# Two layers of spectral mixing and MLP on one core: layer 2's d transform by frequency modulo four, split halves on the way back, and some work on GpSimd

## The chip, the cores and the metric

The kernel runs on one core of a Trainium2 chip. The core has TensorE (PE in the profile; its weight loads are listed as PEld), VectorE (DVE), ScalarE (ACT), GpSimd (POOL) and a queue engine (SP), each with its own instruction stream; they meet only through semaphores. The metric is device time in microseconds, the median of several executions. Matrix products take a stationary operand of 128 columns (a weight load) and stream a moving operand of up to 512 columns past it; results land in PSUM, which has eight banks of 512 fp32 per partition, and DVE or ACT copy them from there to SBUF.

## The reference

One sequence of S = 2048 rows of D = 512 columns in bf16 goes through two identical layers. Each layer is a spectral block and a mixer-MLP block, both with residuals:

```python
def _A_ref(x, w_r, w_i):
    X = jnp.fft.rfft2(x.astype(jnp.float32), axes=(-2, -1))
    X = X * (w_r + 1j * w_i)
    return jnp.fft.irfft2(X, s=(S, D), axes=(-2, -1)).astype(jnp.bfloat16)

def _B_ref(x, w1, w2, w3, w4):
    h = gelu(layernorm(x) @ w1)
    # four column groups of h, shifted by +1, -1, +2, -2 rows: g0..g3
    x1 = x + concatenate([g0, g1, g2, g3]) @ w2
    return x1 + gelu(layernorm(x1) @ w3) @ w4

for layer in range(2):
    x = x + _A_ref(layernorm(x), A_w_r, A_w_i)
    x = x + _B_ref(layernorm(x), B_w1, B_w2, B_w3, B_w4)
```

w1 and w2 are 512x512, w3 is 512x1792, w4 is 1792x512. The spectral weights have 2048x257 entries and are the same in both layers.

## The kernel before

Row 16p+q of x is held in partition p, slot q (`K.x`, 128 x 16 x 512), so the row transform over 2048 points splits into one of 128 points over p and one of 16 points over q. Each layer runs these stages; in brackets is the letter by which an order list calls them.

- Front (O, G): for each slot q the table T, scaled by the row's 1/std (Q, `scaled_T`), is the moving operand and x[:, q] the stationary one. The result, transposed to d on the partitions, goes to V (`take_V`). There are three forms of the matmuls. `over_p_quarters` (line 431) makes eight a row, of 256 and 128 columns, and delivers four combinations of the four quarters of d. `over_p` (413, 415) makes four of 256 columns and delivers the sums and differences of the two halves of d. `over_p_plain` (441) makes four of 128 columns; ACT then copies the right half (`right`) and DVE folds it with the left (`fold_V`, four additions, line 453). Layer 1's front, at the start of the kernel, uses the quarters for all rows. Layer 2's front, in the last part of layer 1, uses the plain form for the first five pairs of rows (PLAIN = 5) and `over_p` for two pairs and two single rows.
- d transform (d, t): `over_d` makes four matmuls for each of 16 blocks b. Layer 1 (lines 549, 551, 555) takes frequencies modulo four, with the table FL: two matmuls of 128 and two of 256 columns. Layer 2 (line 560) takes even and odd frequencies, with the table FA: four of 256 columns. `take_d` copies PSUM to TV on ACT (line 159) or DVE (157). Blocks 2 to 13 go in pairs, 0, 1, 14 and 15 singly (UNITS).
- q transform (q, x): `over_q` (584), and the copy to X by `take_q`. X has two buffers.
- Weights (p): `weigh` (603) multiplies X by the real and imaginary planes of W on DVE, into PB.
- q back (b, m): `back_q` (614), eight matmuls of 128 columns a block, and `take_b`, the copy into M, which lies in hT. Block 15 is copied in two halves by F (the half of the frequencies), all others whole.
- d back (D, Y): `back_d` (632), eight matmuls of 256 columns for a pair of rows, both halves F in one op; `take_D` copies to Y.
- p back (P, a): `back_p` (644), and the sum with x on DVE, which also sums the row (652).
- LN and mixer: squares on ACT (s, line 306), mean and variance on GpSimd (r, lines 312 to 314, then 339 to 343), square root on ACT for the first two groups (e), reciprocal on DVE (i), norm (n, lines 390 on DVE, 392 on ACT), DMA transpose (T, line 672, on SP's queue), w1 (v, 684), gelu (h, 691), w2 with the row shift (u, 700), sum (f, 708), residual add on DVE (E, 715).
- MLP: norm (o), transpose (U), w3 (w, 735), gelu (g, 742), w4 (W, 755), add to x (A, 761), and either statistics for the next layer (B, j, S, J) or the store (y, 765).

Because FA delivers the frequencies in another order, W is permuted between the layers, in place through an X buffer, by 16 ops on DVE (L, `permute`, lines 813 and 814), and the table G is loaded again in the other order (`load_G2`). FL lies in a spare buffer of xT, FA is loaded by SP's queue with the MLP weights.

All work is in program order per engine, written out in three lists: ORDER_0 (layer 1's front), ORDER_A (the rest of layer 1 and layer 2's front), ORDER_B (the rest of layer 2). Each entry is an op letter, its index, an engine letter for flexible ops (V is DVE, A is ACT) and, after a point, the PSUM bank. `Xn` makes n matmuls on zeros (line 278) that leave no result.

Of the kernel before, what the change touches and what calls it, by code (L numbers as in the profile page):

```python
# [12 lines left out]
ALU = mybir.AluOpType  # L13
# [15 lines left out]
def dft_tables():  # L29
# [27 lines left out]
    FA = np.stack([cos, -sin], axis=1).reshape(2, P, 2, P, 2)[..., ::-1].transpose(1, 0, 4, 2, 3)  # L57
# [8 lines left out]
    G = G.transpose(2, 0, 1)  # L66
    G2 = G.reshape(P, 2, 2, D // 2)
    G = G.reshape(2, P, 2, D // 2).transpose(1, 0, 2, 3)
# [30 lines left out]
    out = {"T": np.stack([T, -T], axis=1), "FA": FA, "FL": FL, "TL": TL, "TL2": TL2, "TR": TR, "G": G, "G2": G2,  # L99
# [9 lines left out]
def kernel(  # L109
# [30 lines left out]
    for last in (False, True):  # L140
        layer(K, last)
        if not last:
            K.load_G2()
# [18 lines left out]
def load_all(K, A_x, A_w_r, A_w_i, B_w1, B_w2, B_w3, B_w4):  # L162
# [29 lines left out]
    def load_tables():  # L192
        spare = K.grp.tile([P, 4, 4, P], BF16, name="xT", bufs=4)
        K.FL = spare[:, 0:2].rearrange("p a b c -> p (a b c)")[:, 0:768]
        K.dummy = spare[:, 2, 0:1]
        q.dma_start(K.FL, dram["FL"])
        load_TL(0)
        load_TL(1)
        load_TR(0)
# [14 lines left out]
    def load_G2():  # L214
        for f in range(2):
            nc.sync.dma_start(K.G[:, f], dram["G2"][:, f])

    K.load_G2 = load_G2

    def load_mlp():  # L220
# [8 lines left out]
        K.FA = K.const.tile(list(tabs["FA"].shape), BF16, name="FA")  # L229
        for t in range(2):  # L230
            nc.sync.dma_start(K.FA[:, t], dram["FA"][:, t])

# [48 lines left out]
class Stats:  # L281
# [68 lines left out]
    def invert_twice(self):  # L350
        self.K.nc.vector.reciprocal(self.r[:], self.sd[:])
        self.shift()
# [34 lines left out]
    def apply(self, i, src, dst, eng):  # L387
        r = self.r[:, i:i + 1]
        if eng == "V":
            self.K.nc.vector.tensor_scalar(dst, src, self.mv[:, i, 0:1], r, op0=ALU.add, op1=ALU.mult)  # L390
        else:
            self.K.nc.scalar.activation(dst, src, ACT.Identity, bias=self.mr[:, i, :], scale=r)


def scaled_T(K, q, r, eng="V"):

    K.Tq[q] = K.stream.tile([P, 2, P], BF16, name="Tq", bufs=12)
# [7 lines left out]
def over_p(K, qs, split=False):  # L405

    ps = banks(K, 2 if split else len(qs))
    for i, q in enumerate(qs):
        Tq = K.Tq.pop(q)
        for t in range(2):  # L410
            o = ps[:, t, 0:256] if split else ps[:, i, t * 256:(t + 1) * 256]
            a, z = t * P, 256 + t * P
            K.nc.tensor.matmul(o, lhsT=K.x[:, q, a:a + P], rhs=Tq[:, 0:1].to_broadcast([P, 2, P]), start=True,
                               stop=False)
            K.nc.tensor.matmul(o, lhsT=K.x[:, q, z:z + P], rhs=Tq[:], start=False, stop=True)
    return ps


def over_p_quarters(K, qs, split=False):

    ps = banks(K, 2 if split else len(qs))
    for i, q in enumerate(qs):
        T = K.Tq.pop(q)
        plus, both, swap = T[:, 0], T[:], T[:, ::-1]
        twice = lambda k: T[:, k:k + 1].to_broadcast([P, 2, P])
        for h in range(2):
            o = (ps[:, h, 0:256] if split else ps[:, i, h * 256:(h + 1) * 256]).rearrange("d (k p) -> d k p", k=2)
            terms = ((0, o, twice(0)), (1, o[:, 1], plus), (3, o[:, 1], plus), (2, o, swap)) if h == 0 else \
                    ((1, o, swap), (0, o[:, 0], plus), (2, o[:, 0], plus), (3, o, twice(1)))
            for n, (c, dst, rhs) in enumerate(terms):  # L430
                K.nc.tensor.matmul(dst, lhsT=K.x[:, q, c * P:(c + 1) * P], rhs=rhs, start=(n == 0), stop=(n == 3))  # L431
# [14 lines left out]
def fold_V(K, qs, ps, right):  # L446
    n, lo = len(qs), qs[0]
    v = K.V[:].rearrange("d (t h) b q c -> d h t q b c", h=2)[:, :, :, lo:lo + n]
    left = ps[:, :, 0:256].rearrange("d q (t b c) -> d t q b c", t=2, c=4)
    right = right.rearrange("d q (t b c) -> d t q b c", t=2, c=4)  # L450
    for h, op in ((0, ALU.add), (1, ALU.subtract)):
        for t in range(2):
# [479 lines left out]
```

## Time and profile before

| | |
|---|---|
| three runs | 347.82, 348.92, 348.92 us, median 348.92 |
| span of the profiled execution | 345.6 us |
| the median less that span | 3.3 us |
| PE, PEld, DVE, ACT, POOL busy | 336.6, 190.3, 187.5, 195.5, 62.8 us |
| granted TensorE clock | 1.000 |
| first matmul on x | 8.19 us |
| d transform of layer 1, of layer 2 begins | 19.48, 182.96 us |
| transform back over d begins | 38.05, 202.79 us |
| last addition to x | 342.33 us |

The profile does not give the profiled execution's own device time; it stands here by its span, and the 3.3 us between that span and the median are carried through. Matmuls are pipelined and their records overlap, so a matmul's cost is read from the distance of starts (0.216 us for 512 columns, 0.110 for 256, 0.056 for 128) and not from its listed length. The same holds, less strongly, for ACT and DVE, whose instructions start about 0.1 us before the one in front has ended. A few matmul records are missing (448 of w3's are there, 464 of w4's 476).

### The profile page before, as it was taken

What the parts mean: (1) busy time and instruction counts of PE and PEld (TensorE: products, weight loads), DVE (VectorE), ACT (ScalarE), POOL (GpSimd) and SP (SyncE); (2) the same over time, 40 slices, a digit from 0 to 9 for tenths busy, and PEclk for the clock granted to TensorE, in tenths of its full rate; (3) what the DMA queues carried; (4) which work ended last, traced back from release to release, by engine and by line L of the source; (5) the groups of instructions that cost most, each with busy time, mean ns of one, the idle gap of its engine ahead of it and who ended that gap; (6) DMA issues with size and microseconds to landing.
All of it is one profiled execution on the core that took longest, in us unless ns stands there. A gap on an engine that the chain in (4) does not pass through costs nothing.

```text
span 345.6 us, 5672 instructions
## 1 busy us (share of the span) xinstructions
PE 336.6 (97%) x2161; PEld 190.3 (55%) x2178; DVE 187.5 (54%) x448; ACT 195.5 (57%) x348; POOL 62.8 (18%) x157
## 2 busy tenths in 40 slices
PE   6999999999999999999999999999999999999996
PEld 4978884444444444444577888544444444444443
DVE  5989597668354351178789969757514110211021
ACT  4989899755616616015527979976572344132500
POOL 1460047530301400010000002554014001000000
PEclk9999999999999999999999999999999999999999
DMA  7997975430031210300000002572103060203012
GB/s 259 280 361 236 383 173 101 84 62 0 3 61 21 33 24 14 49 13 1 2 0 2 2 2 44 99 97 41 27 2 61 0 108 0 46 14 95 0 32 76
DMA packets 45834, 25.12 MB, mean 73 GB/s; under 512 B 35008, under 2 KB 42816, under 8 KB 45808
## 3 DMA queue, kind: packets, MB, share of 16 engines
q1 hardware_dynamic: 44336, 20.27, 24.8%
q0 software_dynamic: 1232, 4.40, 3.7%
q8 instruction: 17, 0.28, 0.4%
q10 hardware_dynamic: 240, 0.10, 0.1%
q14 instruction: 9, 0.07, 0.1%
HBM read 12.13 MB, written 2.10 MB: 41 GB/s over the span
## 4 chain that ended last, share of the span: by engine, by line
PE 83%; ACT 7%; DVE 5%; DMA 3%; issue 2%; SPq 0%; ACTq 0%; DVEq 0%
PE ps L735 28%; PE ps L755 28%; PE ps L700 8%; PE ps L684 7%; PE ps L431 3%; PE ps L632 2%; PE ps L614 2%; ACT xn L306 2%; PE ps L644 1%; ACT hT L159 1%; DVE PB L603 1%; PE ps L584 1%; ACT X L159 1%; DVE X L157 1%; DVE x_state L652 1%
## 5 line engine op out<-in xcount | busy, mean ns | idle before, releaser
L742 ACT ACTIVATE gT<-ps 128x1024 bf16<-128x1024 f32 x56 | 56.6, 1023 | 80.4 <-PE ps L735 79.7
L735 PE MATMUL ps<-xT,w 128*128 128x512 bf16 x448 | 99.3, 379 | 0.0
L755 PE MATMUL ps<-w,gT 128*128 128x512 bf16 (+1 forms) x464 | 98.3, 366 | 0.6
L755 PEld LDWEIGHTS <-gT 128*128 128x128 bf16 x476 | 46.5, 98 | 50.1
L735 PEld LDWEIGHTS <-w 128*128 128x128 bf16 x448 | 43.8, 98 | 52.6
L761 DVE TENSOR_TENSOR x_state<-ps,x_state 128x512 bf16<-128x512 f32 (+1 forms) x34 | 22.1, 657 | 86.1 <-PE ps L755 78.9
L708 DVE SCALAR_TENSOR_TENSOR xn<-xn,ln_c,ps 128x512 bf16<-128x512 bf16 x32 | 23.5, 745 | 26.3 <-PE ps L700 19.5
L700 PE MATMUL ps<-w,hT 128*128 128x512 bf16 x123 | 28.8, 379 | 0.3
L684 PE MATMUL ps<-xT,w 128*128 128x512 bf16 x128 | 28.8, 379 | 0.2 <-DMA xT<-xn 0.2
L306 ACT ACTIVATE junk<-xn 128x512 bf16<-128x512 bf16 x32 | 19.9, 622 | 12.7 <-DVE xn L708 12.7
L652 DVE SCALAR_TENSOR_TENSOR x_state<-ps,x_state 128x512 bf16<-128x512 f32 x32 | 20.5, 686 | 4.2 <-PE ps L644 4.1
L294 DVE BATCH_NORM_STATS2 ln_st<-x_state 128x6 f32<-128x512 bf16 (+1 forms) x31 | 20.1, 663 | 3.7 <-DMA x_state<-in_A_x_dram 3.5
L700 PEld LDWEIGHTS <-hT 128*128 128x128 bf16 x128 | 12.4, 98 | 15.3 <-ACT hT L691 0.8
L684 PEld LDWEIGHTS <-w 128*128 128x128 bf16 x128 | 12.3, 98 | 15.3 <-DMA xT<-xn 1.4
L312 POOL TENSOR_SCALAR ln_mv<-ln_s 128x4 f32<-128x4 f32 x16 | 5.7, 357 | 80.3 <-DVE x_state L652 68.7
L306 ACT ACTIVATE xn<-x_state 128x512 bf16<-128x512 bf16 x32 | 20.0, 631 | 0.4 <-DVE x_state L652 0.2
L603 DVE TENSOR_TENSOR PB<-X,W 128x2048 bf16<-128x2048 bf16 (+1 forms) x20 | 19.4, 1010 | 0.2
L691 ACT ACTIVATE hT<-ps 128x512 bf16<-128x512 f32 x32 | 17.4, 604 | 2.5 <-PE ps L684 2.4
L314 POOL TENSOR_TENSOR ln_mv<-ln_s,ln_t 128x4 f32<-128x4 f32 x16 | 3.8, 239 | 80.1 <-ACT junk L306 73.5
L614 PE MATMUL ps<-TR,PB 128*128 128x128 bf16 x256 | 16.3, 219 | 0.1
L159 ACT ACTIVATE TV<-ps 128x1024 bf16<-128x1024 f32 (+1 forms) x16 | 14.2, 914 | 3.8 <-PE ps L560 2.3
L644 PE MATMUL ps<-Y,Tinv 128*128 128x256 bf16 x128 | 15.4, 272 | 0.5 <-ACT Y L159 0.2
(96 smaller groups left out, 388.3 us busy)
## 6 DMA issues: line engine op xcount, KB each, us to landing
w<-in_B_w_dram SPq DMA_DIRECT2D x2, 1792.0 KB, 13.0
W<-W POOLq DMA_DIRECT2D x4, 514.0 KB, 4.7
x_state<-in_A_x_dram SPq DMA_DIRECT2D x8, 256.0 KB, 4.5
out_dram<-x_state SPq DMA_DIRECT2D x15, 128.0 KB, 1.8
w<-in_B_w_dram SPq DMA_DIRECT2D x2, 512.0 KB, 4.8
W<-in_A_w_r_dram SPq DMA_DIRECT2D x7, 128.5 KB, 6.9
W<-in_A_w_i_dram SPq DMA_DIRECT2D x7, 128.5 KB, 6.6
TL<-tab_TL POOLq DMA_DIRECT2D x3, 256.0 KB, 5.1
```

The costliest lines, as they stand in the source:

```text
L159: K.nc.scalar.activation(dst, src, ACT.Copy, bias=0.0, scale=1.0)
L306: K.nc.scalar.activation(out, src, ACT.Square, bias=0.0, scale=D ** -0.5, accum_out=self.s[:, i, 1:2])
L603: nc.vector.tensor_tensor(t, X.pop(u)[:, 0:2 * n].unsqueeze(1).to_broadcast([P, 2, 2 * n, 256]), K.W[:, :, 2 * u:2 * u + 2 * n, 1:257], op ...
L614: nc.tensor.matmul(oh, lhsT=pab[u][:, k, 2 * (b - u) + h, F * P:(F + 1) * P], rhs=K.TR[:, k:k + 2, 2 * b + h], start=(k == 0), stop=(k == 1))
L652: nc.vector.scalar_tensor_tensor(K.x[:, q, :], ps.pop(("P", q)), 1.0, K.x[:, q, :], op0=ALU.mult, op1=ALU.add, accum_out=ln[g].s[:, i, 0:1])
L684: nc.tensor.matmul(o[:, i], lhsT=K.w1[:, t, j * P:(j + 1) * P], rhs=xT[g][:, :, t, :], start=(t == 0), stop=(t == 3))
L700: nc.tensor.matmul(o, lhsT=K.hT[:, j, st:st + P], rhs=K.w2[:, j, :], start=(j == 0), stop=(j == 3))
L708: nc.vector.scalar_tensor_tensor(xn[:, q, :], xn[:, q, :], ln[q // 4].c[:, q % 4:q % 4 + 1], ps.pop(("u", n)), op0=ALU.mult, op1=ALU.add, ...
L735: nc.tensor.matmul(o[:, i], lhsT=K.w3[:, c, t * P:(t + 1) * P], rhs=xT3[g][:, :, c, :], start=(c == 0), stop=(c == 3))
L742: nc.scalar.activation(gT[g][:, 2 * j:2 * j + 2, :], ps.pop(("w", k)), ACT.Gelu_apprx_tanh, bias=0.0, scale=1.0)
L755: nc.tensor.matmul(o, lhsT=gT[g][:, t, i * P:(i + 1) * P], rhs=K.w4[:, t, d], start=(t == 0), stop=(t == 13))
L761: nc.vector.tensor_tensor(x, ps.pop(("W", n)), x, op=ALU.add)
```

## The change

Layer 2 uses layer 1's d transform (FL, frequencies modulo four), so FA, G2, the permutation of W and `load_G2` go, and `over_p` goes with them. FL gets a tile of its own. Layer 2's front makes six pairs plain and the rest in quarters; the fold becomes two subtractions, one sum into a tile `pairs`, and two more operations on DVE or GpSimd (I). The copy of a quarters result may be cut into two halves by block (SPLIT_FIRST, SPLIT_V; L is the second half). Blocks 12 to 15 of the q transform back are cut by F in both layers (SPLIT_B; V and l are the second half), and the transform back over d is two ops, D for F = 0 and C for F = 1. X has three buffers, the scaled tables eight in place of twelve. Seven products (p), nine norms (n), fifteen norms (o), eleven residual adds (E), seven scaled tables (Q) and three folds (I) go to GpSimd (engine letter P). The three order lists are new throughout; idle matmuls are X3 ahead of layer 1's d transform and X6 ahead of layer 2's, where X4 stood ahead of layer 1's transform back, and X3 and X4 ahead of layer 2's d transform. A form of the transform back over d with a fold (K, H, FOLD) is written but not called.

```diff
-    q.dma_start(K.FL, dram["FL"])
+    K.FL = K.const.tile([P, 768], BF16, name="FL")
+    q.dma_start(K.FL[:], dram["FL"])
...
     def apply(self, i, src, dst, eng):
-        if eng == "V":
+        if eng in "VP":
+            e = self.K.nc.vector if eng == "V" else self.K.nc.gpsimd
+            e.tensor_scalar(dst, src, self.mv[:, i, 0:1], r, op0=ALU.add, op1=ALU.mult)
...
-    K.Tq[q] = K.stream.tile([P, 2, P], BF16, name="Tq", bufs=12)
+    K.Tq[q] = K.stream.tile([P, 2, P], BF16, name="Tq", bufs=8)
...
-def fold_V(K, qs, ps, right):
+def fold_V(K, qs, ps, right, pairs):
+    for t in range(2):
+        K.nc.vector.tensor_tensor(v[:, 3 * t], row(ps[:, :, 0:256])[:, t], row(right)[:, t], op=ALU.subtract)
+    K.nc.vector.tensor_tensor(pairs, ps[:, :, 0:256], right, op=ALU.add)
+
+def fold_again(K, qs, pairs, eng):
+    e = K.nc.vector if eng == "V" else K.nc.gpsimd
+    for t, op in ((1, ALU.add), (2, ALU.subtract)):
+        e.tensor_tensor(v[:, t], row[:, 0], row[:, 1], op=op)
...
     def over_d(u):
-            if not last:
...
-            for h in range(2):
-                for t in range(2):
-                    nc.tensor.matmul(oi[:, 1 - h], rhs=K.FA[:, t, h],
-                                     lhsT=V[:, 2 * t + h, 2 * b:2 * b + 2].rearrange("d b q c -> d (b q c)"),
-                                     start=(t == 0), stop=(t == 1))
+            oi = o[:, i].rearrange("p (e r f) -> p e r f", e=2, r=4)
+            part = lambda k: V[:, k, 2 * b:2 * b + 2].rearrange("d b q c -> d (b q c)")
+            nc.tensor.matmul(oi[:, :, 3], lhsT=part(1), rhs=K.FL[:, 0:P].rearrange("p (e f) -> p e f", e=2),
+                             start=True, stop=True)
...
-        X[u] = K.stream.tile([P, 4, 256], BF16, name="X", bufs=2)
+        X[u] = K.stream.tile([P, 4, 256], BF16, name="X", bufs=3)
...
-        nc.vector.tensor_tensor(t, X.pop(u)[:, 0:2 * n].unsqueeze(1).to_broadcast([P, 2, 2 * n, 256]),
+        (nc.vector if eng == "V" else nc.gpsimd).tensor_tensor(t, X.pop(u)[:, 0:2 * n].unsqueeze(1).to_broadcast([P, 2, 2 * n, 256]),
                                 K.W[:, :, 2 * u:2 * u + 2 * n, 1:257], op=ALU.mult)
...
+    def back_d(m, F):
+        if F == 0:
+            ps["D", m] = banks(K, 2)
+        o = ps["D", m]
+        for i in range(2):
+            for e in range(2):
+                nc.tensor.matmul(o[:, i, e * 256:(e + 1) * 256], lhsT=M[:, F, e, 2 * m + i, :], rhs=K.G[:, F, e, :],
+                                 start=(F == 0 and e == 0), stop=(F == 1 and e == 1))
...
-    def permute(k):
...
-TAKE_B = ("FFFFFFFFFFFFFFFB", "FFFFFFFFFFFFFFFB")
+SPLIT_B = ((12, 13, 14, 15), (12, 13, 14, 15))
+SPLIT_FIRST = (5, 6, 7, 8)
+SPLIT_V = (6, 14, 15)
-PLAIN = 5
+PLAIN = 6
...
 ORDER_0 = """
+s0 s1 i0 s4 i1 s5 f2 S0 s6 s7 J0 Q0A Q1A i4 s2 O0.6 i7 i6 S2 s10 J2 i2 Q4V Q5V s9 Q7A s3 O2.0 s11 i3 Q6A s8 S1 f3 J1
...
+i14 G5V S5 L5A G4A O6.4 G6A J5 Q14V O7.6 G7A Q15V O8.7 G3V G8A L7V L8A L6V
 ORDER_A = """
...
+q10.2 d8.4 t14V d15.7 p1P x10A p10P p4V q6.2 d12.0 b3.6 t15V t8A q8.4 x6A b4.2 b2.3 b5.7 p6V t12A x8A m4A q14.0 m3V
...
+V12.0 b12.1 m6A b8.4 m12A p15V b15.7 m11V V14.3 V15.1 m13V m14V m8A V13.5 m15V D0.6 l14A l15V l12A D1.2 l13A C1 C0 Y0V
...
+j12 W15.1 O4.2 I2P A15 S12 B15 J12 j15 G4A G4V W13.5 W14.3 A13 Q12A S15 B13 j13 A14 W24.0 I4P S13 J15 Q15A J13
+O5.2 B14 A24 B24 G5A j14 S14 J14 O15.1 L15A G5V I5V Q13P Q14A G15A O6.4 G6A L6A O14.6 L14A G14A
 ORDER_B = """
+X6.7 d15.2 d1.1 t15V d4.4 t4A q15.6 d8.2 t1V x15V p15P d12.0 t12V q4.4 d2.6 t8A q1.2 q12.0 t2V x4A p4V d10.4 q2.6 x1A
+x12A d0.2 t0V d14.3 b15.0 b4.1 t10A p1P q0.4 x2A b5.2 x0A p0P q8.6 p12V m4A m15A d6.4 p2V x8A b1.1 t14V b2.0 t6A q10.6
+p8V b12.3 m12V q6.4 x10A x6A m2V b9.3 q14.6 x14A b0.0 b3.4 b13.5 b8.6 p10V p6V b11.7 m0A m3A b10.0 m1A m5V m8A m9A
+b6.1 m11V p14P m13V V12.6 m10A b7.2 b14.3 V15.0 m6A V13.7 m14A m7V V14.4 D3.1 l14A D2.3 l13V l15V l12A C3 C2 Y2V D1.5
...
```

## The prediction

> **What bounds the kernel now.** I read the page first (busy shares and the chain that ended last), then the busy time of each engine by stage, then the groups by form for durations, and last the timeline where TensorE pauses. From the page:
>
> ```profile
> span 345.6 us, 5672 instructions
> ...
> PE 336.6 (97%) x2161; PEld 190.3 (55%) x2178; DVE 187.5 (54%) x448; ACT 195.5 (57%) x348; POOL 62.8 (18%) x157
> ...
> PE 83%; ACT 7%; DVE 5%; DMA 3%; issue 2%; SPq 0%; ACTq 0%; DVEq 0%
> ```
>
> TensorE is busy 97% and owns 83% of the chain. So an edit is worth what it takes out of TensorE's stream, plus the pauses of TensorE that it closes; work taken off DVE or ACT pays only where TensorE waits for them. The stages, from the timeline cut into stretches (length, then busy time and count of PE, PEld, DVE, ACT, POOL):
>
> ```profile
> 19.48:38.05 18.57, 18.43 (x260) 15.15 (x260) 17.02 (x22) 17.38 (x27) 3.38 (x6) 1.00 0.90 307
> 178.73:182.96 4.23, 4.15 (x42) 3.38 (x39) 3.97 (x13) 3.38 (x6) 0.00 (x0) 1.00 0.00 0
> 182.96:202.79 19.83, 19.15 (x257) 16.37 (x258) 18.74 (x23) 17.04 (x26) 0.00 (x0) 1.00 0.01 2
> ```
>
> The first is layer 1 from its d transform to the first transform back over d, the third the same stage of layer 2, the second the front of layer 2 after its last W matmul. All three engines are nearly full in both spectral stages. Elsewhere (52.5 to 178.7 and 224 to 342) TensorE runs through, so the 16 W copies on DVE there cost nothing now, and their going gains nothing. Two pauses stand where the transform back over d begins (timeline):
>
> ```profile
> 37.34 0.60 PE L278 MATMUL ps<-zeros 128*128 128x256 bf16 x4
> 38.05 2.79 PE L632 MATMUL ps<-G,hT 128*128 128x256 bf16 x24
> 202.79 2.78 PE L632 MATMUL ps<-G,hT 128*128 128x256 bf16 x24 [0.45 <-ACT hT L159]
> ```
>
> In layer 1 four idle matmuls (0.43 us at 0.108 us each) and 0.28 us pass before L632; in layer 2 it is 0.62 us. Both wait for the last copies into hT.
>
> **The change part by part.** Durations come from this one execution: span 345.6 us; the median of the three runs is 348.92, so 3.3 us lie around the span, which I keep.
>
> *Layer 2's d transform.* The old form is four 256-column matmuls a block: 24 of them start within 2.52 us, 0.110 each, 0.438 a block. The new one is layer 1's, two of 128 and two of 256 columns; in the chain its blocks follow each other every 0.33 us:
>
> ```profile
> 20.17 0.06 PE ps L549
> 20.23 0.06 PE ps L551
> 20.28 0.22 PE ps L555 x2
> 20.50 0.06 PE ps L549
> ```
>
> 16 blocks x 0.108 = -1.73 us. It is collected only if the copies keep up. I count start to start: ACT takes 0.90 us for a 128x1024 copy and 0.48 for 128x512, DVE 1.14 and 0.60, DVE's product 1.14 (two blocks) and 0.61 (one). By the order lists layer 2's stage goes from 17.2 to 15.9 us on DVE and from 16.1 to 15.4 on ACT, TensorE from 19.0 to 17.3 (d 5.3, q 4.2, b 7.8). Layer 1 before carried 16.5 and 17.0 beside 17.3 plus 0.43 of idle matmuls in 18.57 us, so the new stage should fit 18.1 us. Full credit, -1.73; if copies bind, only -1.2.
>
> *Transform back in halves.* L632's work is unchanged, but its first half needs only the first half of blocks 12 to 15, whose four second copies (0.29 to 0.34 us each) now run beside the D matmuls (four take 0.44 us). I take the pauses from 0.71 to 0.2 in layer 1 and from 0.62 to 0.2 in layer 2: -0.9; ends -1.3 (both gone) and 0 (the last first half comes as late as the last whole did).
>
> *Layer 2's front.* Pair 5 moves to the plain form (L441, 0.222 us a row, from 0.44), rows of pair 6 and the two single rows go from 0.44 to the quarters form (L431, 128 in 10.87 us, 0.68 a row): +0.52 on TensorE, and one idle matmul fewer, -0.11. What sets this stretch is the last half row: its add, statistics, square root, reciprocal, scaled table (now on ACT, 0.40, where DVE took 0.20), its matmuls, its copies. Followed by hand, the d transform starts 4.1 us after the last W matmul; now 4.23. I take 0, ends -0.3 and +0.8 (POOL makes row 13's table, queued behind a fold of pair 4; TensorE stands if it is late). The folds of V have 1.4 us more on DVE or POOL; DVE's (2.0 us for pair 5) ends at 3.6 by the same walk, before the copies.
>
> *Layer 1's front.* Both first tables go to ACT (0.40 each) and two more statistics (0.58 each) stand before the reciprocal on DVE, but that now waits less in its queue: first matmul at about 8.25 against 8.19. At the end the copies are cut by blocks, so the first d waits for both column halves: 0.6 us after the last matmul, now 0.51, and three idle matmuls fill it. +0.25; ends 0 and +0.8. The tables for d and q are asked for a little earlier on POOL's queue, still before W's doublings, which wait for W as now.
>
> *Layer 1's spectral stage.* Three products go to POOL (2.35 us of DVE), a third X buffer lets copies run ahead: -0.2, ends 0 and -0.5.
>
> *GpSimd.* It gets 7 products, 9 norms, 11 residual adds, 15 norms before w3, 7 tables and 3 folds. No row shows a two-input product there. The nearest are these, with DVE's own:
>
> ```profile
> L254 POOL TENSOR_SCALAR TL<-TL 128x512 bf16<-128x512 bf16 x1 | 1.7, 1669 | 0.1
> L255 POOL COPY TL<-TL 128x512 bf16<-128x512 bf16 x1 | 0.7, 746 | 0.0
> L603 DVE TENSOR_TENSOR PB<-X,W 128x1024 bf16<-128x1024 bf16 x8 | 5.4, 690 | 0.1
> ```
>
> The copy's rate for 1024 elements gives 1.5 us, the strided scalar's 3.3. A product streams three operands where the copy streams two: 1.5 x 1.5 = 2.2 us for one block, 4.5 for layer 1's product of two. The next b of each comes 3 to 6 us of TensorE's work after it, so the length alone is hidden. What matters is DVE and POOL in each other's way:
>
> ```profile
> 88.52 1.06 POOL L312 TENSOR_SCALAR ln_mv<-ln_s 128x4 f32<-128x4 f32 x1
> ...
> 88.52 0.42 DVE L715 TENSOR_TENSOR x_state<-x_state,xn 128x512 bf16<-128x512 bf16 x1
> 88.85 0.69 DVE L813 COPY X<-W 128x1024 bf16<-128x1024 bf16 x1
> ```
>
> L312 takes 0.24 us alone (at 209.36) and 1.06 here: it ends at 89.58, when DVE's copy does (89.54). So POOL is held by DVE's SBUF-to-SBUF work. The other way round the trace has only tiny POOL operands: beside the 1.11 us power at 50.27 two L390 of DVE keep their 0.33 us step. So DVE's cost lies between 0 and, if it is held for a whole product, 4.6 us of TensorE (worked out below). I take +0.7, near the row in which DVE isn't held. The Trainium skill's SBUF page ("SBUF — State Buffer", section "Who interferes with whom") speaks against this change: a DVE instruction with two SBUF inputs and a GpSimd one that reads SBUF exclude each other for the whole instruction, whoever started first. The row shows one direction of it, no row here the other; by the rule the term is +4.6, and the sum +2.3, 351.2 us.
>
> *Norms on POOL before w1.* n on POOL replaces 0.33 us of DVE by 0.75 to 1.67 (rows above), and stands in the queue ahead of the next group's sums, power and reciprocal inputs. Transposes land 3.2 us after issue and now come just in time (L684 waited 1.4 us in all, on weights). +0.3; ends 0 and +2. In the MLP stages POOL's adds and norms lie beside 50 us of w3 and w4 matmuls: 0. FA's and G2's loads leave SP's queue (FA's held it from 32.46 to 41.80, the first transpose is issued at 47.25), eight T buffers replace twelve: 0. The tail is as now: add 0.42, one 64 KB store.
>
> Sum: -1.73 - 0.9 + 0 + 0.25 - 0.2 + 0.7 + 0.3 = -1.58. Span 344.0, time **347.3 us**.
>
> **The rivals.**
> 1. *DVE is held by POOL's products (slower).* In layer 2 POOL's product of block 1 gets its X about 0.25 us before DVE is free for block 4's: DVE starts 2.0 us late, of which 1.5 reach TensorE at b4; block 8's product then meets block 0's, 1.0 more. In layer 1 the 4.5 us product of blocks 10 and 11 meets DVE's of 4 or 6: about 2.1. Together 4.6 instead of 0.7: +2.3, 351.2 us. It decides from 2.3 us of held time on TensorE's path. For it: POOL is plainly held in the mirror case. Against: the copies out of PSUM beside L254 (17.39 to 19.06) kept 1.13 us a step, and half of DVE's work in the stage is such.
> 2. *POOL's queue makes the statistics late.* Two norms at 1.67 us before a group's sums, in both layers, no cover: +2.0 instead of +0.3, 349.0. For it: L312 to L343 wait for nothing else now. Against: 15 us of D and P matmuls lie there.
> 3. *The d saving isn't collected:* ACT and DVE stay the bound, DVE at 18.74 of 19.83 now. -0.5 in place of -1.73: 348.5. Against: both lose work too.
>
> **How the numbers follow.** A median of this kernel tells 0.3% (1.05 us) from no change. Forecast 0.50, all faster. Rival 1: 0.23, slower. Rival 2: 0.15, about half slower (0.08), half within. Rival 3: 0.12, 0.07 faster with the pauses closed, 0.05 within. Faster 0.57, same 0.12, slower 0.31. The low end: every term at its good end (-1.73 - 1.3 - 0.3 - 0.5 = -3.8) and the run spread of 1.1 give 344.0, cut to 344.4; the high end takes in rival 1 with rival 2's smaller part, 352.0. Forecast alone: 345.2 to 347.9.
>
> **What the changed profile would show.** L546 to L552 for layer 2 at 0.33 us a block, its spectral stage near 18 us instead of 19.83; transform back starting within 0.3 us of the last b; POOL products of 2.2 us. I am wrong where DVE products start only when a POOL product ends, where L-lines of w1 wait for transposes, or where the first matmul is later than 8.3 us.

## The result and the profile after

The changed kernel takes 357.67 us (median of four runs, 357.2 to 358.29), the kernel before 348.37 beside it (347.66 to 348.92): ratio 1.0278, 95% interval 1.0254 to 1.0303. The change makes the kernel slower by 9.3 us, where 1.6 us less was forecast; the time lies outside the range given. The experiments below give each ratio to runs of the kernel before made beside them; their median lies between 347.41 and 348.67, because that kernel's runs fall into two clusters (last section). The span of the profiled execution goes from 345.6 to 355.9 us. From the page of the kernel after:

```profile
span 355.9 us, 5705 instructions
...
PE 339.1 (95%) x2175; PEld 190.0 (53%) x2192; DVE 177.7 (50%) x378; ACT 192.6 (54%) x349; POOL 121.3 (34%) x212
...
PEclk9899899999999999999999999999999999999999
...
PE 73%; DVE 9%; ACT 8%; DMA 4%; POOL 2%; issue 2%; SPq 0%; ACTq 0%; DVEq 0%; POOLq 0%
```

GpSimd's busy time has doubled (62.8 to 121.3 us) and DVE's has fallen by only 9.8, with 378 instructions for 448. TensorE's part of the chain fell from 83 to 73%, DVE's rose from 5 to 9 and GpSimd is on it at all. Two digits 8 stand in the row of TensorE's granted clock, where the kernel before had none. Cut into stages at the same marks as before, in us of the two profiled executions:

| stage | before | after | change |
|---|---|---|---|
| start to the first matmul on x | 8.19 | 9.21 | +1.02 |
| to layer 1's d transform | 11.29 | 12.59 | +1.30 |
| to its first transform back over d | 18.57 | 24.93 | +6.36 |
| to the first w1 | 14.40 | 14.47 | +0.07 |
| to the last w4 | 126.16 | 127.05 | +0.89 |
| to layer 2's d transform | 4.34 | 4.15 | -0.19 |
| to its first transform back over d | 19.83 | 20.26 | +0.43 |
| to the first w1 | 14.65 | 14.99 | +0.34 |
| to the last w4 | 124.59 | 124.73 | +0.14 |
| to the end | 3.54 | 3.49 | -0.05 |

Of the 10.3 us, 8.7 lie ahead of layer 1's transform back over d: 2.3 in the front, 6.4 in the spectral stage. The two spectral stages of the kernel after, in the view of busy time by stretch (length, then busy time and count of PE, PEld, DVE, ACT, POOL, then granted clock, DMA share, GB/s):

```profile
21.80:46.73 24.93, 19.64 (x256) 15.74 (x257) 21.84 (x22) 16.96 (x26) 11.35 (x8) 0.93 0.91 307
192.40:212.67 20.27, 18.30 (x257) 14.21 (x258) 18.31 (x20) 16.37 (x24) 9.80 (x4) 1.00 0.01 2
```

Layer 1's DVE carries the same number of instructions as before (22) and shows 21.84 us of busy time in place of 17.02. Layer 2's has three instructions fewer (20 for 23) and shows 18.31 in place of 18.74. In layer 1 DVE's instructions have become longer, in layer 2 fewer of them take nearly the same time. The timeline of layer 1 says which (start, duration, engine, line, operation, what it waited for in brackets):

```profile
30.06 0.68 DVE L152 CAST TV<-ps 128x512 bf16<-128x512 f32 x1
30.20 3.85 POOL L583 TENSOR_TENSOR PB<-X,W 128x2048 bf16<-128x2048 bf16 x1 [2.28 <-ACT X L154]
30.66 4.48 DVE L583 TENSOR_TENSOR PB<-X,W 128x2048 bf16<-128x2048 bf16 x1
...
35.23 1.02 ACT L154 ACTIVATE X<-ps 128x1024 bf16<-128x1024 f32 x1 [4.20 <-DVE PB L583]
...
36.29 1.23 DVE L583 TENSOR_TENSOR PB<-X,W 128x2048 bf16<-128x2048 bf16 x1 [0.55 <-ACT X L154]
36.30 2.72 PE L594 MATMUL ps<-TR,PB 128*128 128x128 bf16 x24 [3.77 <-ACT X L154]
```

GpSimd's product of blocks 10 and 11 runs from 30.20 to 34.05. DVE's product of the next pair starts 0.46 us after it and ends at 35.14, 1.09 us after GpSimd's has ended; alone such a product takes 1.23 (at 36.29), so it can have done next to nothing until then. In the changed kernel five two-block products of DVE start inside one of GpSimd, and all five end 1.08 to 1.09 us after it. ScalarE's copy of the next X waits 4.20 us for DVE's product, and the b matmuls wait 3.77 us for the copies. Then the matmuls themselves run at half rate (same view as the stages; the clock is the third column from the end):

```profile
30.20:36.30 6.10, 2.34 (x32) 1.77 (x32) 5.55 (x4) 1.91 (x3) 3.85 (x1) 0.98 0.76 216
36.30:39.10 2.80, 2.80 (x26) 2.59 (x27) 1.82 (x2) 2.36 (x4) 0.00 (x0) 0.50 1.04 398
```

The 24 b matmuls among these 26 start 0.107 us apart, where 128 columns take 0.056 at full clock. The record of the clock has 0.5 for 36.01 to 39.43, and for 8.71 to 12.12 in the front. So there are three things to separate: GpSimd's products holding DVE, the halved clock, and the new orders by themselves. The theory was that the first two, with a late reciprocal in the front, carry the loss. The rivals were that the orders (three X buffers, blocks in another sequence) are slow on their own, and that the new d transform is worth nothing.

The Trainium skill states the hold in "SBUF — State Buffer", section "Who interferes with whom": a VectorE instruction with two SBUF inputs and a GpSimd instruction that reads SBUF shut each other out for the whole instruction, and the one issued first wins. The rows agree with it: 4.48 us in place of 1.22. They also agree with its exception, that VectorE work with at most one input in SBUF isn't held unless it runs in a two-port mode: the copy at 30.06, whose input lies in PSUM, keeps its 0.68, and so does one at 203.78, in the middle of a GpSimd product.

### The profile page after: what moved, and what is told of

Its sections match the earlier page's. It is cut to its first block, busy times and chain, and to the rows that moved or that the text cites. A ratio compares the mean times of both kernels' runs of the same rounds, so it can differ in the third digit from the quotient of the medians.

```text
span 355.9 us, 5705 instructions
## 1 busy us (share of the span) xinstructions
PE 339.1 (95%) x2175; PEld 190.0 (53%) x2192; DVE 177.7 (50%) x378; ACT 192.6 (54%) x349; POOL 121.3 (34%) x212
## 4 chain that ended last, share of the span: by engine, by line
PE 73%; DVE 9%; ACT 8%; DMA 4%; POOL 2%; issue 2%; SPq 0%; ACTq 0%; DVEq 0%; POOLq 0%
PE ps L753 27%; PE ps L733 23%; PE ps L682 8%; PE ps L698 5%; PE ps L404 3%; DVE PB L583 3%; PE ps L594 2%; DMA xT<-xn 2%; ACT xn L290 2%; ACT junk L290 2%; DMA x_state<-in_A_x_dram 1%; PE ps L614 1%; PE ps L552 1%; DVE x_state L650 1%; DVE xn L706 1%
## 5 line engine op out<-in xcount | busy, mean ns | idle before, releaser
L740 ACT ACTIVATE gT<-ps 128x1024 bf16<-128x1024 f32 x56 | 55.7, 1021 | 87.0 <-PE ps L733 86.9
L583 POOL TENSOR_TENSOR PB<-X,W 128x1024 bf16<-128x1024 bf16 (+1 forms) x7 | 18.4, 2626 | 23.3 <-DVE X L152 12.8
L594 PE MATMUL ps<-TR,PB 128*128 128x128 bf16 x256 | 18.1, 228 | 6.1 <-ACT X L154 3.8
L583 DVE TENSOR_TENSOR PB<-X,W 128x2048 bf16<-128x2048 bf16 (+1 forms) x13 | 22.9, 1782 | 0.8 <-ACT X L154 0.8
L594 PEld LDWEIGHTS <-PB 128*128 128x128 bf16 x256 | 15.9, 102 | 8.6 <-DVE PB L583 5.5
L154 ACT ACTIVATE X<-ps 128x1024 bf16<-128x1024 f32 (+1 forms) x16 | 13.6, 864 | 8.7 <-DVE PB L583 5.7
L404 PE MATMUL ps<-Tq,x_state 128*128 128x256 bf16 (+1 forms) x160 | 15.0, 259 | 3.0 <-DMA x_state<-in_A_x_dram 3.0
```

The source lines that it names most:

```text
L583: (nc.vector if eng == "V" else nc.gpsimd).tensor_tensor(t, X.pop(u)[:, 0:2 * n].unsqueeze(1).to_broadcast([P, 2, 2 * n, 256]), K.W[:, :, ...
L594: nc.tensor.matmul(o[:, k0 * P:(k0 + 1) * P], lhsT=pab[u][:, k, 2 * (b - u) + h, f * P:(f + 1) * P], rhs=K.TR[:, k:k + 2, 2 * b + h], star ...
L740: nc.scalar.activation(gT[g][:, 2 * j:2 * j + 2, :], ps.pop(("w", k)), ACT.Gelu_apprx_tanh, bias=0.0, scale=1.0)
```

## Experiments

**Products back on DVE.** The change with its seven GpSimd products moved.

```
-... d15.7 p1P x10A p10P ...  p14P ...        (layer 1)
+... d15.7 p1V x10A p10V ...  p14V ...
-... x15V p15P ... p1P ... p0P ... p14P ...   (layer 2)
+... x15V p15V ... p1V ... p0V ... p14V ...
```

> The changed kernel with its seven GpSimd products given back to DVE at the same places of the list, nothing else. Theory held (a GpSimd product keeps DVE's two-input products waiting until it ends): no DVE product over 1.3 us, layer 1's spectral stage falls from 24.9 us (21.80 to 46.73) to about 19, layer 2's from 20.3 to about 18.5, the clock dip at 36 us goes, time about 350 us (-7.5). Rival order (the new lists themselves starve TensorE in these stages): DVE has 4.2 us more work there, the stages stay above 23 and 20 us, time 356 to 358. The late first matmul (9.21 us) and the clock dip after it stay under both.

Measured: 351.19 us, ratio to the kernel before 1.0086 (1.0053 to 1.0119), so 6.5 us of the loss go. Layer 1's spectral stage falls from 24.93 to 19.25, with no halved clock in it; layer 2's from 20.26 to 20.00 only, which misses the 18.5 expected. The stretches of this run:

```profile
23.24:42.48 19.24, 18.14 (x256) 14.35 (x257) 18.41 (x25) 17.28 (x27) 2.76 (x5) 1.00 0.86 295
188.16:208.15 19.99, 18.36 (x256) 14.21 (x257) 18.27 (x24) 16.24 (x24) 0.00 (x0) 1.00 0.01 2
```

In layer 2 DVE now carries four products more (24 instructions for 20) and is busy for the same 18.3 us as with the products on GpSimd. What GpSimd took from it, it gave back in waiting. So in layer 2 the products on GpSimd neither cost nor bring more than 0.3 us; in layer 1 they cost 5.7, the halved clock after them included. The miss in layer 2 left the question why the saving of the d transform does not appear even then.

**One product of the kernel before on GpSimd.** The reverse: nothing of the change but the product of blocks 10 and 11 of layer 1.

```
-        nc.vector.tensor_tensor(t, X.pop(u)...
+        (nc.gpsimd if u == 10 and not last else nc.vector).tensor_tensor(t, X.pop(u)...
```

> The kernel before with one product, layer 1's for blocks 10 and 11, moved to GpSimd, nothing else. Theory held: DVE's next product (blocks 6 and 7), which follows it at once, takes about 4.5 us in place of 1.22, ACT's next copy to X waits for it as there are two X buffers, TensorE pauses 2 to 4 us, time about 351 (+2.5), more with a clock dip. Rival order: DVE is relieved of 1.1 us in a stage that it bounds, time 347.5 to 348.5.

Measured: 353.33 us, ratio 1.0147 (1.0115 to 1.0179). Layer 1's spectral stage goes from 18.57 to 23.94, +5.4, and the median lies 4.7 above that of the kernel before; the theory had 2.5 without the halved clock. Its timeline:

```profile
28.23 3.85 POOL L603 TENSOR_TENSOR PB<-X,W 128x2048 bf16<-128x2048 bf16 x1 [3.20 <-ACT X L159]
28.74 4.42 DVE L603 TENSOR_TENSOR PB<-X,W 128x2048 bf16<-128x2048 bf16 x1
...
34.35 1.05 PE L614 MATMUL ps<-TR,PB 128*128 128x128 bf16 x16 [2.75 <-DVE hT L157]
```

The same picture in another order: held from 28.74 to 32.08, then TensorE waits 2.75 us, and a halved stretch follows from 36.41 to 39.83. One moved product, with 1.22 us of DVE work in it, costs the stage 5.4 us here, and its own result kept nobody waiting: no wait of this run is put down to it. Since nothing else is changed, the hold and its sequel are shown to cost this much without the new orders.

**The reciprocal ahead of two statistics.** In the front of the kernel after, rows 6 and 7 of x land at 7.27 us; their statistics stand ahead of the reciprocal that the first scaled table needs, which therefore comes at 8.48. From the timeline of the kernel after:

```profile
7.27 1.29 DVE L278 BATCH_NORM_STATS2 ln_st<-x_state 128x6 f32<-128x512 bf16 x2 [0.54 <-DMA x_state<-in_A_x_dram]
...
8.48 0.15 DVE L368 RECIPROCAL ln_r<-ln_r 128x2 f32<-128x2 f32 x1
...
8.66 0.91 ACT L386 ACTIVATE Tq<-T,ln_r 128x256 bf16<-128x256 bf16 x2 [1.18 <-DVE ln_r L368]
...
9.21 0.58 PE L404 MATMUL ps<-Tq,x_state 128*128 128x256 bf16 x3 [3.01 <-DMA x_state<-in_A_x_dram]
```

The timeline puts TensorE's wait down to x, but ScalarE makes the first two tables only from 8.66 to 9.57, and the first matmul follows the first of them.

```
-s0 s1 i0 s4 i1 s5 f2 S0 s6 s7 J0 Q0A Q1A i4 ...
+s0 s1 i0 s4 i1 s5 f2 S0 J0 Q0A Q1A s6 s7 i4 ...
```

> The changed kernel with group 0's reciprocal and both scaled tables ahead of the statistics of rows 6 and 7. Theory queue (the reciprocal stands behind statistics whose rows land at 7.27): first matmul at 8.2 to 8.3 us in place of 9.21, the pause before it 2.1 us, the clock stays at 1.0 between 8.7 and 12.1, layer 1's d transform begins at about 19.6 in place of 21.80, time about 355.4 (-2.3). Rival landing (the front is bound by the landing of x whatever the order): d transform begins within 0.5 us of 21.80.

Measured: 356.78 us, ratio 1.0232 (1.0203 to 1.026). The first matmul on x comes at 8.47 instead of 9.21, a little later than expected. The gain is 0.9 us and not 2.3, because the pause before it is still followed by a halved stretch (8.17 to 11.58). That pause is 2.70 us; a pause of TensorE at the start is counted here from the start of the last idle matmul plus its 0.110 us, which gives about 0.17 more than the timeline lists. The d transform starts 0.64 us earlier (21.16).

**Forty idle matmuls instead of 27** in the kernel after, which fill most of its pause of 3.18 us and change nothing else.

> The changed kernel with 40 idle matmuls at the start in place of 27: they end at about 7.6 us, so the pause before the first matmul (9.21) is 1.6 us in place of 3.18; no work moves. Theory clock (the pause halves the granted clock for 3.41 us): the clock stays at 1.0 from 8.7 to 12.1, the 32 matmuls of 9.2 to 13.2 take 2.7 us and not 4.0, time about 356.3 (-1.3). Rival: the dip at 8.7 comes from the start of the program, not from the pause, and stays; time 357.7.

Measured: 356.67 us, ratio 1.0214 (1.0169 to 1.026). The pause is 0.96 us, the front has no halved stretch, and the d transform starts 1.22 us earlier (20.58). Half of that is lost again in layer 1, where the halved clock after GpSimd's product now lasts two stretches (34.14 to 40.97) and the spectral stage takes 25.60. The four runs spread widely, from 353.81 to 357.07.

**The three mends together:** products on DVE, the reciprocal first, 40 idle matmuls.

> The changed kernel with three edits together: every product on VectorE, the reciprocal and the two scalings of the first pair ahead of the statistics of rows 6 and 7, and 40 idle matmuls instead of 27. If the loss came from the three causes seen singly (products of GpSimd, the late reciprocal, the halved clock after a long TensorE pause), they add up: first matmul on x at 8.4 to 8.6 us, no stretch of halved clock before the middle of layer 1, the d transform of layer 1 from 19.5 to 20.0, spectral stages 19.2 and 20.0, median 347.5 to 349.5. If the causes overlap, so that one takes the place of another, 350 to 352.

Measured: 350.58 us, ratio 1.0083 (1.0062 to 1.0104); the causes overlap, as the second case had it. Now the first matmul on x comes at 8.22, the clock is full everywhere, and still the front takes 12.31 us to the d transform (before 11.29), layer 1's spectral stage 19.25 (18.57) and layer 2's 20.00 (19.83). 3.2 us of the loss belong neither to GpSimd's products nor to the clock. In the two profiled executions 1.0 of this lies in the front, 0.85 in the two spectral stages and 2.0 in the two MLPs (127.39 for 126.16, 125.34 for 124.59), of which 0.44 is the pair of rows that the change moves there; other stages give back some tenths.

**The same with the old order of the first front** (and 27 idle matmuls, the last pair alone copied in halves).

```
-s0 s1 i0 s4 i1 s5 f2 S0 J0 Q0A Q1A s6 s7 i4 s2 O0.6 ...
+s0 s1 s3 i1 i0 s2 s4 i3 i2 S0 J0 Q0V s5 i4 S1 J1 Q1A O0 s6 s7 ...
```

> The run with the three edits, with the order of layer 1's front of the kernel before (the statistics' and scalings' order, the last pair alone in halves, 27 idle matmuls), Tq in eight buffers. If the new order of the front costs the 1.0 us that remained there (12.31 us from the first matmul on x to the d transform against 11.29), it goes: d transform at 19.5, median 349.2 to 349.8. If the d transform's blocks in the new order or the eight buffers are the cause, the 12.3 us stay.

Measured: 349.61 us, ratio 1.0061 (1.0037 to 1.0085). Three of its four runs, with a mean clock of 1.00, lie at 349.26 to 349.66, 1.0 us under the run before: the new order of the front, with its copies in halves, costs about that much. The profiled execution is the fourth, 350.87; it has a halved stretch from 7.82, and its front takes 12.60 us, so a front of 11.3 us was not read directly. It is concluded from the times alone.

**All that the change put on GpSimd back on DVE:** the three mends, and the norms, residual sums, tables and second folds on DVE. GpSimd keeps the small operations of the statistics, as in the kernel before.

> The run with the three edits, and all else that the change put on GpSimd (norms, residual sums, tables, second folds) on VectorE too. If GpSimd's use of the port costs in the MLP and in the transforms back (126.16 became 127.05 and 14.65 became 14.99 us), 0.5 to 0.9 us less than that run. If VectorE has too much work by then, 0.5 to 2 us more, with TensorE waiting for VectorE at the norms of the MLP.

Measured: 360.48 us, ratio 1.037 (1.0343 to 1.0396), 9.9 us more than with them on GpSimd. Layer 1's MLP goes from 127.39 to 131.00, layer 2's front from 4.15 to 6.53, layer 2's MLP from 125.34 to 128.28. The new orders count on GpSimd there. This doesn't show that GpSimd's small operations cost nothing; it shows that in these orders DVE can't take them.

**The d transform alone,** in the kernel before with its orders. Pairs 5 and 6 and the two single rows use the quarters form.

```
-        ps["O", k] = over_p_plain(K, qs) if k < PLAIN else over_p(K, qs, k >= 14)
+        ps["O", k] = over_p_plain(K, qs) if k < PLAIN else over_p_quarters(K, qs, k >= 14)
...
-            oi = o[:, i].rearrange("p (e h f) -> p h e f", e=2, h=2)      (four matmuls on FA)
+            oi = o[:, i].rearrange("p (e r f) -> p e r f", e=2, r=4)      (layer 1's form on FL)
```

> The kernel before with one part of the change: layer 2's d transform by frequency modulo four (FL instead of FA, the second fold on VectorE, quarters in place of halves for the last four pairs, W not permuted, no G2); queues and orders else as before, no work moved to GpSimd. If the saving of TensorE work is collected, layer 2's spectral stage falls from 19.83 to 18.1 to 18.5 us and the median is 346.6 to 347.4. If the copies out of PSUM or VectorE set the stage's pace, it stays at 19.0 to 19.9 and the median is 348.0 to 349.0.

Measured: 349.57 us, ratio 1.0059 (1.004 to 1.0077): slower. Its front and its spectral stage of layer 2, by the view of stretches:

```profile
178.73:184.14 5.41, 5.41 (x66) 4.82 (x63) 4.56 (x13) 3.60 (x6) 0.00 (x0) 1.00 0.00 0
184.14:203.47 19.33, 17.91 (x257) 15.19 (x257) 18.09 (x21) 17.10 (x26) 0.00 (x0) 1.00 0.01 2
```

Against the kernel before, TensorE's busy time in the spectral stage falls by 1.24 us, the stage by 0.50. DVE is busy 18.09 of 19.33 us, 94%, as it was before (18.74 of 19.83). The front pays 1.07 us for it, all of it TensorE's own work (4.26 to 5.41): the quarters form costs more columns than the halves, and with the old orders these six rows stand behind the last W step. The remaining loss in this profile, 1.1 us in layer 2's MLP, is a wait of 1.25 us of w1 for a transpose; the two kernels below that add the halves or cut the products have a longer MLP by as much, the one with the earlier front has not, and its cause was not followed.

**And the transform back in halves,** for blocks 14 and 15 of both layers, on top of that.

```
-b15.2 m13A m14A X4.0 m15A m15V D1.5 Y1A D0.0 Y0A
+b15.2 m13A V14.3 V15.4 m14V m15V X3.0 D1.5 l14A l15V D0.0 C1 Y1A C0 Y0A
```

> The run of the d transform alone, and the transform back over d in halves for blocks 14 and 15 in both layers (first halves of two pairs of rows ahead of the second halves). If the halves are worth what the prediction gave them, the two waits ahead of the transform back lose 0.3 to 0.5 us each: 0.5 to 0.9 us less than the run without the halves. If the wait only moves behind the first halves, no difference over 0.3 us.

Measured: 350.04 us, ratio 1.0083 (1.0055 to 1.0111), no gain. From the start of the last b matmul to that of the first D matmul 1.06 us pass in layer 1 (0.77 in the kernel before, idle matmuls in between in both) and 0.60 in layer 2 (0.67). After that the D matmuls run through, first halves and second halves alike, so the wait has not moved behind the first halves: the first halves themselves come no earlier. In the changed kernel, where four blocks are split, TensorE goes into the D matmuls in both layers with no pause that the timeline lists:

```profile
45.95 0.88 PE L594 MATMUL ps<-TR,PB 128*128 128x128 bf16 x12
46.73 1.47 PE L614 MATMUL ps<-G,hT 128*128 128x256 bf16 x12
...
211.34 1.49 PE L594 MATMUL ps<-TR,PB 128*128 128x128 bf16 x20
212.67 1.04 PE L614 MATMUL ps<-G,hT 128*128 128x256 bf16 x8
```

With its products on DVE the same distances are 0.26 and 0.17 us. So the form with four blocks, in its orders, closes the pauses nearly, and the form with two blocks leaves them.

**Half of layer 2's products left out,** in the kernel before and with the d transform alone, to see whether DVE's lack of room keeps the saving.

```
+        z = 1 if last else 2
+        nc.vector.tensor_tensor(t[:, 0:z], X.pop(u)... K.W[:, 0:z, ...
-  lhsT=pab[u][:, k, 2 * (b - u) + h, ...
+  lhsT=pab[u][:, 0 if last else k, 2 * (b - u) + h, ...
```

> The kernel before with half of layer 2's spectral products left out: VectorE multiplies with the first plane of W only, and the transform back reads that half for both (the output lacks the second plane; TensorE's work and all copies are unchanged). VectorE's 18.74 us in layer 2's spectral stage fall to about 14.1 (six products of 1.22 to 0.68, four of 0.69 to 0.42). If TensorE set that stage's pace, it stays near 19.83 and at most 0.4 us go; if the copies and products of VectorE and ScalarE did, it falls to TensorE's busy 19.15 and some 0.3 of waits, 19.2 to 19.5. Read against the next run.

> The run of the d transform alone with the same half of layer 2's products left out. If the saving of the d transform was not collected because VectorE (18.09 of 19.33 us) and ScalarE (17.10) have no room, it is collected now: layer 2's spectral stage 18.0 to 18.5, that is 1.0 to 1.3 below the kernel before with half products, where with whole products it was 0.50 below. If something else keeps it (order, banks, TensorE's weight loads), the difference stays at 0.5 and the stage at 18.8 or more.

Measured: 347.39 us, ratio 0.9991 (0.9975 to 1.0007), and 348.94 us, ratio 1.0035 (1.0018 to 1.0053). Layer 2's spectral stage with half the products, in the kernel before and then with the d transform alone:

```profile
183.31:202.66 19.35, 18.76 (x257) 16.24 (x257) 15.00 (x23) 16.82 (x26) 0.00 (x0) 1.00 0.01 2
...
184.14:202.73 18.59, 17.69 (x257) 15.24 (x257) 14.44 (x21) 16.87 (x26) 0.00 (x0) 1.00 0.01 2
```

With the d transform alone DVE drops to 14.44 us, the stage from 19.33 to 18.59; in the kernel before, the same cut takes the stage from 19.83 to 19.34. So relief of DVE brings both stages down by 0.5 to 0.7, and the d transform is then worth 0.75 us instead of 0.50. That is half way: not the 1.0 to 1.3 of the theory, nor the unchanged 0.5 of its rival. So DVE's load keeps part of the saving. The stages are read from one execution each; the medians go the same way (the kernel with the d transform is 2.2 us slower with whole products, 1.6 with half). What keeps the rest is open; ScalarE is still busy 91% of the stage (16.87 of 18.59), which speaks for the copies, but no run relieved it.

**The d transform alone with an earlier front:** pair 5 plain too, pairs 4 and 5 moved ahead of the last W step.

```
-... Q10 S15 J15 W13.3 ... W24.4 ... O4.6 O15.2 G4A ... O5.4 G5A O6.1 ...
+... Q10 S15 J15 O4.0 W13.3 G4A ... O5.6 G4V W24.4 G5A ... G5V ... O15.2 ... O6.0 ...
```

> The run of the d transform alone with its front mended: rows 12 and 13 take the plain form too and are transformed before the last W step of the MLP, as in the changed kernel, so that two pairs fewer stand behind it. The d transform of layer 2 then starts 4.2 to 4.6 us after the last W step instead of 5.41, for 0.44 more in the MLP: 0.3 to 0.8 us less than the run of the d transform alone, median 346.8 to 348.2 against 347.4 of the kernel before. If the second folds make VectorE late, the stretch keeps its 5.4 us.

Measured: 353.03 us, ratio 1.0135 (1.0101 to 1.017), a clear miss. In the profiled execution (353.89) the two folds of pair 5 stand on DVE ahead of the last rows' residual sum, statistics and reciprocal (reciprocal at 186.32), TensorE waits 3.12 us for their scaled table, a halved stretch follows, and the front of layer 2 takes 8.72 us. Two of the six runs, at a full mean clock, take 350.9, so the order loses time without the halved clock too. The changed kernel, which has three of the second folds on GpSimd and most of the last tables on ScalarE, takes 4.15 us for this stretch. No version with the new d transform came under the kernel before.

**Idle matmuls in the kernel before:** 40, and 20, in place of 27. Nothing else differs, so the pause ahead of the first matmul on x alone is shorter or longer.

> The kernel before with 40 idle matmuls instead of 27. By the rule read from the profiles so far (stretches of 3.41 us on a fixed raster; one in which TensorE was busy 0.40 or less is followed by one at half clock, one at 0.47 or more is not), the pause ahead of the first matmul on x falls from 1.97 to about 0.6 us, so no raster can find 0.40: no halved stretch in any run, all runs within 0.5 us of one another at 347.0 to 347.5, the upper cluster of the kernel before (348.7 to 349.0) missing. If the pause has nothing to do with it, the runs lie in the same two clusters.

> The kernel before with 20 idle matmuls instead of 27: the pause ahead of the first matmul on x is 2.7 to 2.9 us, and some stretch of the raster holds 0.15 to 0.4 of busy time in most runs: a halved stretch at 8 to 10 us in most or all runs, and a median of 348.6 to 349.2, the upper cluster of the kernel before. If the pause has nothing to do with it, the median stays at 347.4.

Measured: 347.34 us with 40, ratio 0.9984 (0.9972 to 0.9996), all twelve runs between 347.08 and 347.60; 348.78 us with 20, ratio 1.0034 (1.0022 to 1.0047). Beside them the kernel before had 18 of 23 runs at 347.27 to 348.19 and 5 at 348.65 to 348.93. With 40 the upper cluster is gone, as expected, and the median lies 0.2 us under that of the kernel before. Its timeline from 4 us on (13 of the 40 idle matmuls lie ahead of that), with the last idle matmuls 0.9 us ahead of the first real one:

```profile
3.76 3.60 PE L278 MATMUL ps<-zeros 128*128 128x256 bf16 x27
8.22 0.98 PE L431 MATMUL ps<-Tq,x_state 128*128 128x256 bf16 x10 [0.86 <-DMA x_state<-in_A_x_dram]
```

With 20 the median is where it was expected, and 8 of the 12 runs have the mean clock of one halved stretch (0.994 to 0.995), but the profiled execution shows another way there: its clock record begins only at 13.15 us, and until then 32 matmuls of 256 and 128 columns take 5.03 us. They start 0.213 and 0.107 us apart, where full clock gives 0.110 and 0.056; the 20 idle ones ahead of them, of 256 columns, start 0.213 apart too. There the clock had not risen at all by the first matmul, rather than risen and fallen.

## Why the prediction was wrong

*The term for GpSimd holding DVE* is the step that failed most: +0.7 taken, "near the row in which DVE isn't held". That row (DVE's norms beside a 128x4 power) had operands too small to tell, and the bound's upper end, +4.6, stood for a DVE that is held for the whole product, which is what the page "SBUF — State Buffer" of the Trainium skill states. Both the page's rule and the mirror row (GpSimd held by DVE) pointed there, and I weighed a row about operands of four elements above them. The changed kernel shows the difference: DVE's norms keep their 0.41 us beside a 128x4 power, and seven of them grow beside a 128x512 operation (last section). The measured price is 5.7 us in layer 1 (products on DVE: 24.93 to 19.25) and 0.3 in layer 2. Rival 1 had the mechanism with the right place in layer 1, priced at 2.1 there and 2.5 in layer 2. Two things were missing in its price. It held back one DVE product but not what ScalarE and TensorE lose by it: TensorE waited 3.77 us instead of 2.1. And it had no halved clock. A stretch of 3.41 us at half rate in which TensorE is busy 0.91 costs 1.55 us. In layer 2 its price was too high, because what DVE waits there it also saves in products.

*Product lengths on GpSimd:* 2.2 us for one block and 4.5 for two were estimated; started ahead of DVE's they take 1.9 and 3.85, and 2.8 to 2.9 when started inside a DVE product. The estimates were good; the conclusion that "the length alone is hidden" was true and beside the point.

*Layer 1's front,* +0.25 taken, +2.32 measured. "That now waits less in its queue" is the step that failed: the reciprocal waits for rows 6 and 7, which land at 7.27, and their two statistics. That made 1.02 us. The other 1.3 come after the first matmul. With the first matmul back at 8.22 and the clock full, the front still takes 1.02 us longer than before; the old order in the same kernel removes 1.0 of time. So the order costs about 1.0 us in any case. The halved stretch took 1.2 in the run that removed it alone. The two overlap in the changed kernel, and I can't split the 2.3 us further.

*Layer 2's d transform,* -1.73 taken with "full credit" because "the new stage should fit 18.1 us". The stage took 20.26, 20.00 with the products on DVE, and 19.33 in the old order: -0.50 at best, exactly the figure of rival 3. TensorE's work did fall (by 1.24 us with the old order). The step that failed compared each engine's load with the stage's length and took three engines that are "nearly full" for enough room. With half of DVE's products gone, the transform is worth 0.75: DVE's load of 94% keeps part of the saving, and the rest is open. The bound "if copies bind, only -1.2" was itself too hopeful.

*The new orders of the spectral stages:* -0.2 taken for layer 1's third X buffer. With all products on DVE the stage is 0.68 us longer than before, and layer 2's 0.67 longer than the d transform alone in the old order. The orders were written around products that GpSimd was to take; what in them costs this was not taken apart.

*Transform back in halves:* pauses from 0.71 and 0.62 us to none in the changed kernel, -1.3 where -0.9 was taken. There the stages are slow for other reasons; with the products on DVE 0.20 and 0.11 remain, -1.0, which fits the term. Two blocks in the old orders gained nothing, so that the halves alone do it isn't shown. The gain is part of the two spectral stages and vanishes in their loss.

*Layer 2's front:* 0 taken; 4.34 became 4.15, but 0.44 us of its work moved into the MLP: +0.25 in all, within its ends. *Norms on GpSimd before w1:* +0.3 taken, 0.07 and 0.34 measured, right. *MLP:* 0 taken; +0.89 in layer 1, of which 0.44 is that moved pair and 0.47 a pause at 95.6 us (0.30 in the timeline's list). Shortly before it GpSimd's and DVE's residual sums start 0.25 us apart and DVE's takes 1.37 us in place of 0.42:

```profile
92.85 1.33 POOL L713 TENSOR_TENSOR x_state<-x_state,xn 128x512 bf16<-128x512 bf16 x1
93.10 1.37 DVE L713 TENSOR_TENSOR x_state<-x_state,xn 128x512 bf16<-128x512 bf16 x1
...
96.31 1.02 PE L733 MATMUL ps<-xT,w 128*128 128x512 bf16 x4 [0.30 <-ACT gT L740]
```

That the hold makes this pause is only argued: TensorE waits for ScalarE's gelu, and no run took this pair of sums apart.

Two of the three signs named beforehand came true: "the first matmul is later than 8.3 us", and "DVE products start only when a POOL product ends" in substance, since the trace lists the start at once and the wait as a longer product. The third, w1 waiting for transposes, did not (0.4 us in all).

## What to carry to other kernels

Before work goes to GpSimd, look at what DVE does with two SBUF operands in the same microseconds: a 3.85 us product on GpSimd cost DVE 3.2 us and the stage 5.4 in the kernel before, although GpSimd had nothing else to do there and the product's result wasn't late. A saving on TensorE in a stage where DVE and ScalarE are nearly full (here 94 and 86%) may come in only in part (here 0.5 of 1.24 us), so price it by relieving them in an experiment before the stage's order is rewritten. And a pause of TensorE like those of 2 to 4 us here has to be priced twice, for itself and for the halved clock that may follow.

## What the runs showed of the hardware

*The clock falls after a stretch, not after a pause.* In every profile that has one, the halved clock after a full one comes in stretches of 3.413 us or two of them, on a raster that is fixed within a run (after: 8.706 and 36.013 lie eight stretches apart) and different from run to run. I worked out TensorE's busy share of each stretch of that raster from the matmul records. Stretches at full clock with 0.00, 0.22, 0.24, 0.27, 0.31, 0.35 and 0.40 of busy time were followed by one at half clock. Those with 0.47 (twice), 0.48, 0.50, 0.51 and more were not. In a halved stretch 0.66 and 0.67 kept the clock down for another, 0.82 and more brought it back. So the same pause can cost 1.4 us or nothing, by where the raster happens to lie: one of 2.70 us with the reciprocal first was followed by a halved stretch, one of 2.71 with the d transform alone was not. This accounts for why the kernel before, whose pause of 1.97 us sits at the edge, has two clusters of times 1.4 us apart at mean clocks of 1.00 and 0.994 (one halved stretch in 346 us makes 0.995), and why 13 more idle matmuls remove the upper one. The Trainium skill's "TensorE: Matmul & The Clock Gate" (Part 1) gives the same free-running window of 3413 ns; its advice under "Why this matters for your kernels", no idle gaps over about 3 us, is too loose for this case, where pauses of 2.21 us (the earlier front) and 2.70 were followed by a halved stretch.

*The hold goes both ways and takes one-input operations with it.* GpSimd's one-block product takes 1.90 us started first (198.00) and 2.89 started inside DVE's (202.75); DVE's two-block products beside them:

```profile
198.00 1.90 POOL L583 TENSOR_TENSOR PB<-X,W 128x1024 bf16<-128x1024 bf16 x1 [0.77 <-ACT X L154]
198.21 2.77 DVE L583 TENSOR_TENSOR PB<-X,W 128x2048 bf16<-128x2048 bf16 x1
...
201.51 2.35 DVE L583 TENSOR_TENSOR PB<-X,W 128x2048 bf16<-128x2048 bf16 x2
202.75 2.89 POOL L583 TENSOR_TENSOR PB<-X,W 128x1024 bf16<-128x1024 bf16 x1 [2.85 <-ACT X L154]
```

Seven norms on DVE (0.41 us) beside GpSimd's sums and norms grew to 0.59 to 1.03 and ended 0.14 to 0.15 us after GpSimd's operation (at 80.07 one takes 1.02, beside a sum from 79.62 to 80.94). Others kept their 0.41, and GpSimd's norm beside them took 0.99 in place of 0.77 (231.13). So an operation with one wide SBUF input and one output holds and is held as well.
